# A transformer block with its gradients on one core: a written order for SP's queue, other places for weight loads, and q's row bound made earlier

## The chip, the core and the metric

The kernel runs on one core of a Trainium2 chip. The metric is device time in microseconds from launch to end; lower is better. The program is one launch with all inputs and outputs in device memory. A profiled execution gives, beside its own time, a span: from its first to its last instruction.

## What is computed

The reference is a block with attention beside a gated feed-forward part, and all of its gradients:

```
xn = layernorm(x)                                   # x: 1 x 2048 x 512
q, k, v = split(xn @ wqkv)                          # 32 heads of 16
s = softmax(q k^T / 4) v, heads joined, @ wo
b = gelu(layernorm(xn) @ w1 + b1) @ w2 + b2         # 512 -> 1792 -> 512
out = x + s * silu(b)
returns out and the gradients of x, wqkv, wo, w1, b1, w2, b2 for a given grad_out
```

Data are bfloat16. Gelu is the tanh form. No maximum is subtracted from the scores as they come: each row of q gets a bound, minus the root of (its squared norm times the largest squared norm of a k row of that head), which is put into an extra column of q so that the score matmul subtracts it.

## The kernel before, in words

The work has three parts: a part before attention (`phase_pre`, L42 to L481), attention forward and backward together (`attention_core`), and the remaining gradients (`phase3`). The change touches only the first and its hand-over to the second.

**Data.** The 2048 rows are 16 tiles of 128 rows; four tiles are a group. Group g is loaded as one 128 x 4 x 512 tile. Tiles are named as in the code: x4 (input), xn4 (normalized), y4 (normalized twice), xnT and yT (their transposes), NS (k and v), NQ (q, with an extra column for the bound), KPad and QPad (padded copies that are transposed for attention), ND (grad_out-side operand of attention), h1p (before Gelu), hgT (after it), dso4 (gradient that enters attention), gB (gate and its gradient), do4 (grad_out).

**Stages, in the order of TensorE.** (1) Layer norm, and per tile the projections to k, v and q (`kv_tile`, 12 matmuls). The transposes xnT of groups 0 and 1 are made by TensorE (`turn_xn`), those of groups 2 and 3 and all yT by DMA transposes on SP's queue (L134, L163). ScalarE (ACT) copies the results out of PSUM. (2) For groups 0 and 1, `h_tile(g, fc)`: 14 tiles of 4 matmuls each, with the bias added by VectorE (DVE, L267) for even fc and for 5 and 11, by ACT (L269) for the others; every second tile ACT applies Gelu (L271) and two stores are issued on SP's queue: H1T_s (L272) and HGT_s (L273). (3) `m_group(0)`: per row tile 14 matmuls with w2 (L282), then on DVE and ACT the gate: m = result + b2 (L286), tanh and sigmoid (L289, L290), gB and dso (L294, L295; dso reads do4), and three operations more (L304 to L309), with a store of gB by GpSimd (POOL, L310). At the end of a group dso4 is transposed by DMA (L299) and stored. `m_group` begins with `load_do`, the load of do4, of which there is one buffer. (4) `h_tile` of group 2, with `do_proj` (a matmul with wo's transpose, cast by ACT to ND, L346) behind its last four tiles; m_group(1); the same for group 3; m_group(2). The last group's m, and the do_proj of groups 2 and 3, are left over: `left_over` hands them out as steps that stand in the first block of attention.

PSUM has seven banks in this part, shared by all matmul results (`psA`, tag "mm"); one more is the pool `psz`.

**Norms and the bound.** `norms` squares a tile on POOL (L174, two buffers named sq) and sums it on DVE (L175): `k_norm` for k in stage 1, `q_norm` for q in the h stages (after fc 2, 4, 6, 8, 10, 12 of group 1; 1, 3, 5, 6, 8, 9 of group 2; 1, 3, 5, 6 of group 3). The maximum over all k rows is made in h of group 0: DVE reduces over tiles (L453), then POOL over partitions (`partition_all_reduce`, L454). Then `row_shift1` multiplies the norms (L434, L435; after fc 9 of group 3), `row_shift2` takes the root on ACT (L439; after its last fc), and `row_shift3` writes NQ's column, copies it to QPad on POOL and transposes (`turn_q`, L426), behind h of group 3.

**What sets the order.** Inside a `tc.manual_schedule(engines=...)` block, the named engines run their instructions in the order of the code. In both blocks of `phase_pre` these are TensorE, ACT, DVE and POOL. SP, which only issues DMAs, is not among them: its order is chosen by the framework's scheduler, which may put an instruction ahead of others that stand before it in the code. Each queue works strictly in order; an instruction that waits for a semaphore holds up what is behind it. In the built program SP's order is: x(0), x(1), w2, the transpose of wo, b1, XN_s(0), x(2), XN_s(1), x(3), and then the stage's transposes and stores in the code's order; the transpose of KPad (L460) and the loads of b2 and do (group 0) come before the first H1T_s; the loads of do for groups 1 and 2 come five DMAs ahead of the last HGT_s of the h stage before them. ACT's queue issues the loads of wqkv (two parts) and w1 at the start.

Of the kernel before, what the change touches and what calls it, by code (L numbers as in the profile page):

```python
# [9 lines left out]
f32 = mybir.dt.float32  # L10
# [26 lines left out]
def rows4(a, g):  # L37

    return a[g * 512:(g + 1) * 512].rearrange("(p t) d -> p t d", t=4)


def phase_pre(ctx, tc, k, A_x, A_wqkv, A_wo, B_w1, B_b1, B_w2, B_b2, grad_out, opnds, psz, tailp):  # L42
# [25 lines left out]
    nc.vector.memset(half[:], 0.5)  # L68
    kmaxrun = wts.tile([128, H], f32, name="kmaxrun")
    kmax2 = wts.tile([128, H], f32, name="kmax2")  # L70

    yT, hgT = {}, {}
    c2 = c1.enter_context(ExitStack())
    p1 = pool(c2, "pre_p1", 2)
    wqkv_sb = p1.tile([128, IC, 3 * D], bf16, name="wqkv_sb", bufs=1)
# [4 lines left out]
    def load_x(g):  # L80
        x4[g] = p1.tile([128, 4, D], bf16, name="x4", bufs=2)
        if g == 0:
            for h in range(2):
                nc.sync.dma_start(out=x4[g][64 * h:64 * h + 64], in_=rows4(x2, g)[64 * h:64 * h + 64])
        else:
            nc.sync.dma_start(out=x4[g][:], in_=rows4(x2, g))

# [82 lines left out]
        nc.scalar.activation(out=dst, in_=ps[:].rearrange("p (a j c) -> p a j c", a=NPAIR, j=2), func=ACT.Copy, scale=0.25 if c0 == 0 else 1.0)  # L170

    def norms(pl, dst, src):
        sq = pl.tile([128, H, DH], f32, name="sq", bufs=2)
        nc.gpsimd.tensor_tensor(out=sq[:].rearrange("p (a j) c -> p a j c", j=2), in0=src, in1=src, op=ALU.mult)  # L174
        nc.vector.reduce_sum(out=dst, in_=sq[:], axis=AX.X)  # L175

# [20 lines left out]
    def k_norm(g, i):  # L197
        norms(p1, kn2[:, 4 * g + i, :], NS[g][:, :, i, :, 1:17])

    with tc.manual_schedule(engines={ET_.PE, ET_.Activation, ET_.DVE, ET_.Pool}):  # L200
        for g in range(2):
            load_x(g)
        nc.scalar.dma_start(out=wqkv_sb[:, :, D:3 * D], in_=wq3[:, :, D:3 * D])
        nc.scalar.dma_start(out=wqkv_sb[:, :, 0:D], in_=wq3[:, :, 0:D])
        nc.scalar.dma_start(out=w1_sb[:], in_=B_w1.rearrange("(c p) f -> p c f", p=128))
        for g in range(4):
            NS[g] = p1.tile([128, NPAIR, 4, 2, NATW], bf16, name="NS", bufs=4)
            nc.gpsimd.memset(NS[g][:, :, :, :, 0:1], 1.0)
        open1(0)
        open1(1)  # L210
        one_a(0, 0)
        for i in range(4):
            one_a(*divmod(i + 1, 4))
            one_b(0, i)
            turn_xn(0, i)
        load_x(2)
        for i in range(4):
            if i < 3:
                one_a(1, i + 1)
            one_b(1, i)  # L220
            if i == 3:
                n2_a(0)
            kv_tile(0, i)
            turn_xn(1, i)
        load_x(3)
        for h4 in range(4):
            permuted_kv(h4)
        steps = [(root2, 0), (n1_a, 2), (n2_b, 0), (kv_tile, 1, 0), (root1, 2), (n2_c, 0, 0), (n2_c, 0, 1), (n1_b, 2),
                 (kv_tile, 1, 1), (n2_c, 0, 2), (n2_c, 0, 3), (n2_a, 1), (kv_tile, 1, 2), (root2, 1), (n1_a, 3), (n2_b, 1),
                 (kv_tile, 1, 3), (root1, 3), (n1_b, 3), (n2_c, 1, 0), (n2_c, 1, 1), (kv_tile, 2, 0), (n2_a, 2), (n2_c, 1, 2),  # L230
                 (n2_c, 1, 3), (kv_tile, 2, 1), (root2, 2), (k_norm, 0, 0), (k_norm, 0, 1), (n2_b, 2), (kv_tile, 2, 2),
                 (n2_c, 2, 0), (n2_c, 2, 1), (k_norm, 0, 2), (k_norm, 0, 3), (n2_a, 3), (kv_tile, 2, 3), (n2_c, 2, 2),
                 (n2_c, 2, 3), (root2, 3), (n2_b, 3), (kv_tile, 3, 0)] + [(k_norm, 1, i) for i in range(4)]
        steps += [(n2_c, 3, 0), (n2_c, 3, 1), (kv_tile, 3, 1), (k_norm, 2, 0), (k_norm, 2, 1), (n2_c, 3, 2), (n2_c, 3, 3),
                  (kv_tile, 3, 2), (k_norm, 2, 2), (k_norm, 2, 3), (k_norm, 3, 0), (k_norm, 3, 1), (kv_tile, 3, 3), (k_norm, 3, 2), (k_norm, 3, 3)]
        for f, *a in steps:
            f(*a)
# [2 lines left out]
    p2 = pool(c1, "pre_p2", 2)  # L240
    h1ps = [p2.tile([128, 2, 512], bf16, name="h1p", bufs=6)]
    w2_sb = k.Oall[:].rearrange("p t d -> p (t d)")[:, 0:FC * D].rearrange("p (c d) -> p c d", c=FC)
    nc.sync.dma_start(out=w2_sb, in_=B_w2.rearrange("(c p) d -> p c d", p=128))
    nc.sync.dma_start_transpose(out=woT, in_=A_wo)
    qn2 = p2.tile([128, NT, H], f32, name="qn2", bufs=1)
    b2_bf = p2.tile([128, D], bf16, name="b2_bf", bufs=1)
    nc.sync.dma_start(out=b2_bf[:], in_=B_b2.rearrange("(o d) -> o d", o=1).to_broadcast([128, D]))
    nc.gpsimd.tensor_copy(out=b2f[:], in_=b2_bf[:])
    nc.sync.dma_start(out=b1_bf[:], in_=B_b1.rearrange("(c p) -> p c", p=128))
    nc.gpsimd.tensor_copy(out=b1c[:], in_=b1_bf[:])  # L250
    ND, dsoT, dso4, do4 = {}, {}, {}, {}

    def h_tile(g, fc):
# [96 lines left out]
    def do_done(g):  # L350
        ts = slice(4 * g, 4 * g + 4)
        nd0 = ND[g][:, 0].rearrange("p t (j c) -> p t j c", j=2)
        nc.gpsimd.tensor_copy(out=QPad[:, ts, 2:4, 0:16], in_=nd0)
        if g >= 2:
            turn_q(g)
        nc.sync.dma_start(out=k.NATQd_s[g], in_=ND[g])
        nc.gpsimd.tensor_copy(out=OP0["NATQd"][:, ts], in_=nd0)

    def left_over(big, mid2, xt2, st2):
# [60 lines left out]
            steps[2 * n + 3][0].append((rest2, t))  # L420
        for g, f in ((8, (do, 8)), (9, (do, 10)), (10, (turn, 0)), (11, (do, 12)), (12, (do, 14))):
            steps[g][1].append(f)
        return steps

    def turn_q(g):
# [15 lines left out]
    def row_shift3():  # L441
        for ts in (slice(0, 4), slice(4, 16)):
            nc.vector.tensor_scalar(out=NQ[:, :, ts, :, 0], in0=qn2[:, ts].rearrange("p t (a j) -> p a t j", j=2), scalar1=-1.0, scalar2=None,
                                    op0=ALU.mult)
            nc.gpsimd.tensor_copy(out=QPad[:, ts, 0:2, 0:17], in_=NQ[:, 0, ts])
            turn_q(ts.start // 4)
        nc.gpsimd.tensor_copy(out=OP0["NATQq"][:], in_=NQ[:, 0])

    with tc.manual_schedule(engines={ET_.PE, ET_.Activation, ET_.DVE, ET_.Pool}):
        for fc in range(FC):  # L450
            h_tile(0, fc)
            if fc == 5:
                nc.vector.reduce_max(out=kmaxrun[:], in_=kn2[:].rearrange("p t h -> p h t"), axis=AX.X)  # L453
                nc.gpsimd.partition_all_reduce(kmax2[:], kmaxrun[:], channels=128, reduce_op=bass_isa.ReduceOp.max)  # L454
        qn = list(range(NT))
        for fc in range(FC):
            h_tile(1, fc)
            if fc in (2, 4, 6, 8, 10, 12):
                q_norm(qn.pop(0))
        nc.sync.dma_start_transpose(out=OP0["KVT"][:].rearrange("r (m k) -> r m k", m=16), in_=KPad[:].rearrange("q k s c -> q (k s c)"))  # L460
        m_group(0)
        for g in (2, 3):
            for fc in range(FC):
                h_tile(g, fc)
                if g == 3 and fc == 9:
                    row_shift1()
                if g == 3 and fc == FC - 1:
                    row_shift2()
                if fc >= 10:
                    do_proj(4 * (g - 2) + fc - 10)  # L470
                elif fc in (1, 3, 5, 6) or fc in (8, 9) and g == 2:
                    q_norm(qn.pop(0))
            if g == 2:
                m_group(1)
        e_one = p2.tile([128, 1], f32, name="e_one", bufs=1)
        nc.scalar.activation(out=e_one[:], in_=k.eps_t[:], func=ACT.Exp)
        row_shift3()
        m_group(2)
        nc.sync.dma_start(out=k.NATQq_s, in_=NQ[:].rearrange("p a t j c -> p a (t j c)"))
    c1.close()  # L480
# [806 lines left out]
```

## Time and profile before

| | |
|---|---|
| time, median of 3 runs | 2342.68 us (2340.48 to 2344.0) |
| the profiled execution | 2337.01 us, of which the span is 2335.1 us |
| PE busy (matmul) | 2228.5 us, 95% of the span |
| DVE, ACT, POOL busy | 2024.3, 2043.9, 315.3 us |
| before attention (to TensorE's first score matmul) | 166.7 us |
| granted TensorE clock, mean | 0.988 |
| DMA traffic | 415.56 MB, 178 GB/s |

How to read it: the busy times overlap, since the engines run side by side. A line of a timeline has the start in us from the beginning of the span, the time taken, the engine, the line of the code, the operation, what is written and read, the count of equal instructions merged and, in brackets, how long the engine stood idle before and what ended that. An engine's name with a q (SPq) is its queue, where DMAs are issued; their landing comes later. "DMA share" is the mean busy share of the 16 DMA engines; values over 1 are edges of stretches. The profiled execution lies 5.7 us under the median of the runs.

### The profile page before, as it was taken

How to read it: one execution, taken by the hardware profiler on the slowest of the kernel's cores; microseconds unless marked ns; L12 is line 12 of the kernel's file. 1: busy time of each engine (PE TensorE's matmuls, PEld its weight loads, DVE VectorE, ACT ScalarE, POOL GpSimd, SP SyncE). 2: the span in 40 equal slices, each digit the busy share in tenths (PEclk: the TensorE clock that was granted, in tenths of full speed). 3: DMA queues.
4: the chain of work that ended last, by engine and by line, in shares of the span. 5: the costliest groups of instructions: out<-in, count | busy, mean ns of one | idle time of the engine just before them, and what ended most of it. 6: DMA issues, size and time to landing. Idle time of an engine off the chain costs nothing.

```text
span 2335.1 us, 50892 instructions
## 1 busy us (share of the span) xinstructions
PE 2228.5 (95%) x20082; PEld 795.2 (34%) x20128; DVE 2024.3 (87%) x3601; ACT 2043.9 (88%) x2329; POOL 315.3 (14%) x758
## 2 busy tenths in 40 slices
PE   7888999999999999999999999999999998889698
PEld 3333333333333333333333333333333333334344
DVE  6577999999999999999999999999999996775164
ACT  6566999999999999999999999999999998883143
POOL 4321111111111111111111111111111112100000
PEclk9999999999999999999999999999999999999899
DMA  9788999999999999999999999999999898796961
GB/s 295 228 279 176 170 179 163 187 157 186 164 180 164 181 165 177 170 173 178 167 180 162 186 162 180 168 179 164 178 169 176 159 157 221 192 214 123 184 163 64
DMA packets 1315362, 415.56 MB, mean 178 GB/s; under 512 B 1272241, under 2 KB 1291698, under 8 KB 1313970
## 3 DMA queue, kind: packets, MB, share of 16 engines
q1 hardware_dynamic: 1311362, 401.56, 90.7%
q0 software_dynamic: 2176, 7.34, 0.9%
q8 instruction: 157, 2.57, 0.4%
q10 hardware_dynamic: 1584, 3.41, 0.4%
q14 instruction: 83, 0.68, 0.1%
HBM read 46.52 MB, written 49.03 MB: 41 GB/s over the span
## 4 chain that ended last, share of the span: by engine, by line
PE 77%; DVE 10%; ACT 3%; issue 3%; DMA 3%; SPq 2%; POOL 0%; DVEq 0%; ACTq 0%; POOLq 0%
PE d L916 12%; PE X L953 11%; PE s L894 11%; PE Z L1034 9%; PE X L966 7%; DVE gts L933 5%; PE Z L1026 5%; PE t L906 5%; PE ET L878 5%; PE XT L978 2%; PE ps_dw L661 1%; PE X L956 1%; PE ps_dhg L676 1%; PE ps_dy L716 1%; PE ps_dwkv L766 1%
## 5 line engine op out<-in xcount | busy, mean ns | idle before, releaser
L933 DVE TENSOR_TENSOR gts<-d,et 128x512 bf16<-128x512 f32 x2048 | 1322.0, 684 | 71.4 <-PE d L916 22.0
L922 ACT ACTIVATE et<-s 128x1024 bf16<-128x1024 f32 x1024 | 1044.6, 1046 | 8.8 <-PE d L916 7.5
L927 ACT ACTIVATE e<-t 128x1024 bf16<-128x1024 f32 x832 | 867.5, 1043 | 23.1 <-PE t L906 5.4
L916 PE MATMUL d<-QDT,KVT 32*128 32x512 bf16 x2048 | 756.5, 384 | 18.7 <-DVE gts L933 17.5
L894 PE MATMUL s<-QDT,KVT 32*128 32x512 bf16 x2048 | 398.3, 384 | 4.8 <-ACT et L922 2.7
L1034 PE MATMUL Z<-gk,W 128*32 128x512 bf16 x2048 | 397.1, 384 | 0.0
L953 PE MATMUL X<-et,Lc 128*32 128x512 bf16 x2048 | 370.1, 389 | 0.0
L956 PE MATMUL X<-et,NAT 128*32 128x512 bf16 x2048 | 368.9, 388 | 0.0
L966 PE MATMUL X<-gts,NAT 128*17 128x512 bf16 x2048 | 330.5, 381 | 0.0
L906 PE MATMUL t<-KVT,QDT 32*128 32x512 bf16 x1664 | 323.7, 384 | 0.9 <-ACT e L927 0.9
L1026 PE MATMUL Z<-e,W 128*32 128x512 bf16 x1664 | 321.6, 383 | 2.7 <-DVE ob L1053 1.2
L916 PEld LDWEIGHTS <-KVT 32*128 32x128 bf16 x2048 | 173.2, 91 | 235.1 <-issue 234.7
L894 PEld LDWEIGHTS <-KVT 32*128 32x128 bf16 x2048 | 105.9, 91 | 249.1 <-issue 229.3
L1000 POOL TENSOR_TENSOR W<-NATQd,rL 128x128 bf16<-128x128 bf16 x64 | 25.7, 401 | 1120.8 <-DVE rL L999 1120.8
L1034 PEld LDWEIGHTS <-W 128*32 128x32 bf16 x2048 | 100.3, 95 | 172.5 <-issue 142.0
L906 PEld LDWEIGHTS <-QDT 32*128 32x128 bf16 x1664 | 92.5, 91 | 146.1 <-issue 141.0
L1026 PEld LDWEIGHTS <-W 128*32 128x32 bf16 x2048 | 105.2, 94 | 105.7 <-issue 96.6
L953 PEld LDWEIGHTS <-Lc 128*32 128x32 bf16 x2048 | 83.6, 93 | 162.3 <-issue 162.2
L883 DVE COPY eE<-ET 128x1024 bf16<-128x1024 bf16 x192 | 130.1, 678 | 4.4 <-PE ET L878 4.4
L878 PE MATMUL ET<-ident_bf,et 128*128 128x128 bf16 x1536 | 119.1, 220 | 2.1 <-DVE e L286 2.1
L878 PEld LDWEIGHTS <-et 128*128 128x128 bf16 x1536 | 86.5, 98 | 45.6 <-issue 45.6
L966 PEld LDWEIGHTS <-NAT 128*17 128x17 bf16 x2048 | 79.6, 89 | 59.4 <-issue 42.8
(197 smaller groups left out, 2328.6 us busy)
## 6 DMA issues: line engine op xcount, KB each, us to landing
gk<-gts SPq DMA_TRANSPOSE x512, 4.5
H1T_s<-h1p SPq DMA_DIRECT2D x28, 256.0 KB, 4.2
h<-H1T_s SPq DMA_DIRECT2D x28, 256.0 KB, 3.3
HGT_s<-hgT SPq DMA_DIRECT2D x21, 256.0 KB, 4.4
NAT_s<-NS SPq DMA_DIRECT2D x4, 1056.0 KB, 5.9
dKVT_s<-ob SPq DMA_DIRECT2D x16, 256.0 KB, 3.6
gb<-GB_s SPq DMA_DIRECT2D x4, 1024.0 KB, 5.8
Rkv<-dKVT_s SPq DMA_DIRECT2D x2, 2048.0 KB, 14.1
```

The source lines that it names most:

```text
L878: nc.tensor.transpose(ET[:, hj, m * 128:(m + 1) * 128], st_et[g - 3 + m][:, hj, 384:512], ident_bf[:])
L894: nc.tensor.matmul(s[:, hj, :], lhsT=op["KVT"][r, kb * 128:(kb + 1) * 128], rhs=op["QDT"][r, qc * 512:(qc + 1) * 512], start=True, stop=Tr ...
L906: nc.tensor.matmul(t[:, hj, :], lhsT=op["QDT"][r, q0:q0 + 128], rhs=op["KVT"][r, kc * 512:(kc + 1) * 512], start=True, stop=True, tile_pos ...
L916: nc.tensor.matmul(d[:], lhsT=op["KVT"][r, kb * 128:(kb + 1) * 128], rhs=op["QDT"][r, qc * 512:(qc + 1) * 512], start=True, stop=True, til ...
L922: nc.scalar.activation(out=et[:], in_=st_s.pop(g)[:], func=ACT.Exp)
L927: nc.scalar.activation(out=e[:], in_=st_t.pop(g)[:], func=ACT.Exp)
L933: nc.vector.tensor_tensor(out=gts[:, g % 2, hj], in0=st_d.pop((g, hj))[:], in1=st_et[g][:, hj], op=ALU.mult)
L953: nc.tensor.matmul(X[64 + 32 * hj:96 + 32 * hj, :], lhsT=Lc[:, :], rhs=et[:, hj, :], start=(kb == 0), stop=False, skip_group_check=True, t ...
L956: nc.tensor.matmul(X[32 * hj:32 * hj + 32, :], lhsT=NATt[:, kb, hj, 1:33], rhs=et[:, hj, :], start=(kb == 0), stop=(kb == 15), tile_positi ...
L966: nc.tensor.matmul(X[64 + 32 * hj:64 + 32 * hj + 17, :], lhsT=NATt[:, kb, hj, 0:17], rhs=gts[:, kb % 2, hj, :], start=False, stop=(kb == 1 ...
L1026: nc.tensor.matmul(Z[32 * hj:32 * hj + 32, :], lhsT=blk[j]["W1"][:, qb, hj, :], rhs=e[:, hj, :], start=(qb == 0), stop=False, tile_positio ...
L1034: nc.tensor.matmul(cur["Z"][32 * hj:32 * hj + 32, :], lhsT=blk[j]["W2"][:, qb, hj, :], rhs=grhs, start=False, stop=(qb == 3), tile_positio ...
```

## The change

SP joins the engines with a written order, in both blocks. Its instructions therefore stand in the order of the code, and the code moves several of them. x(0) is loaded as its first row tile and the other three, no longer as two halves of the partitions. wqkv comes as three parts, in the order k, v, q; w1 and b1 are asked for in the middle of stage 1; w2 on ACT's queue at the head of the second block's code; b2 behind tile 1 of h of group 0; wo's transpose right before m_group(0); KPad's right before m_group(1).

The maximum of k's squares over partitions is made by TensorE in three steps behind fc 5, 8 and 11 of group 0 (`k_max`): a transpose, a reduction and a diagonal matrix on DVE, and a matmul with ones that spreads the 32 maxima over all partitions. POOL's reduction goes.

The q norms move: after fc 0 to 3 and 5 to 8 of group 2, and 0 and 1 of group 3. `row_shift1`, 2 and 3 now stand behind fc 3, 5 and 9 of group 3; of `row_shift3` only the first four tiles are transposed there, and `do_done` transposes those of the other groups. The first sq of this part is allocated at its head. In the first block of attention, the last step gets two fills of two matmuls each, whose results nobody reads.

In the built program w2's load stands on ACT's queue behind the second root of stage 1. do for group 0 stands behind HGT_s of h of group 1's last pair and wo's transpose; do for group 1 behind the last HGT_s of group 2, NATQd_s and KPad's transpose; do for group 2 behind the last HGT_s of group 3, a transpose of QPad and NATQd_s.

```diff
@@ -68,8 +68,12 @@
     nc.vector.memset(half[:], 0.5)
     kmaxrun = wts.tile([128, H], f32, name="kmaxrun")
     kmax2 = wts.tile([128, H], f32, name="kmax2")
-
-    yT, hgT = {}, {}
+    kmd = wts.tile([H, H], f32, name="kmd")
+    kmt = wts.tile([H, 1], f32, name="kmt")
+    ones_h = wts.tile([H, 128], f32, name="ones_h")
+    nc.gpsimd.memset(ones_h[:], 1.0)
+
+    yT, hgT, sqs = {}, {}, []
     c2 = c1.enter_context(ExitStack())
     p1 = pool(c2, "pre_p1", 2)
     wqkv_sb = p1.tile([128, IC, 3 * D], bf16, name="wqkv_sb", bufs=1)
@@ -80,8 +84,8 @@
     def load_x(g):
         x4[g] = p1.tile([128, 4, D], bf16, name="x4", bufs=2)
         if g == 0:
-            for h in range(2):
-                nc.sync.dma_start(out=x4[g][64 * h:64 * h + 64], in_=rows4(x2, g)[64 * h:64 * h + 64])
+            for ts in (slice(0, 1), slice(1, 4)):
+                nc.sync.dma_start(out=x4[g][:, ts], in_=rows4(x2, g)[:, ts])
         else:
             nc.sync.dma_start(out=x4[g][:], in_=rows4(x2, g))
 
@@ -170,7 +174,7 @@
         nc.scalar.activation(out=dst, in_=ps[:].rearrange("p (a j c) -> p a j c", a=NPAIR, j=2), func=ACT.Copy, scale=0.25 if c0 == 0 else 1.0)
 
     def norms(pl, dst, src):
-        sq = pl.tile([128, H, DH], f32, name="sq", bufs=2)
+        sq = sqs.pop() if sqs else pl.tile([128, H, DH], f32, name="sq", bufs=2)
         nc.gpsimd.tensor_tensor(out=sq[:].rearrange("p (a j) c -> p a j c", j=2), in0=src, in1=src, op=ALU.mult)
         nc.vector.reduce_sum(out=dst, in_=sq[:], axis=AX.X)
 
@@ -197,12 +201,11 @@
     def k_norm(g, i):
         norms(p1, kn2[:, 4 * g + i, :], NS[g][:, :, i, :, 1:17])
 
-    with tc.manual_schedule(engines={ET_.PE, ET_.Activation, ET_.DVE, ET_.Pool}):
+    with tc.manual_schedule(engines={ET_.PE, ET_.Activation, ET_.DVE, ET_.Pool, ET_.SP}):
         for g in range(2):
             load_x(g)
-        nc.scalar.dma_start(out=wqkv_sb[:, :, D:3 * D], in_=wq3[:, :, D:3 * D])
-        nc.scalar.dma_start(out=wqkv_sb[:, :, 0:D], in_=wq3[:, :, 0:D])
-        nc.scalar.dma_start(out=w1_sb[:], in_=B_w1.rearrange("(c p) f -> p c f", p=128))
+        for v in (1, 2, 0):
+            nc.scalar.dma_start(out=wqkv_sb[:, :, v * D:(v + 1) * D], in_=wq3[:, :, v * D:(v + 1) * D])
         for g in range(4):
             NS[g] = p1.tile([128, NPAIR, 4, 2, NATW], bf16, name="NS", bufs=4)
             nc.gpsimd.memset(NS[g][:, :, :, :, 0:1], 1.0)
@@ -223,6 +226,9 @@
             kv_tile(0, i)
             turn_xn(1, i)
         load_x(3)
+        nc.scalar.dma_start(out=w1_sb[:], in_=B_w1.rearrange("(c p) f -> p c f", p=128))
+        nc.sync.dma_start(out=b1_bf[:], in_=B_b1.rearrange("(c p) -> p c", p=128))
+        nc.gpsimd.tensor_copy(out=b1c[:], in_=b1_bf[:])
         for h4 in range(4):
             permuted_kv(h4)
         steps = [(root2, 0), (n1_a, 2), (n2_b, 0), (kv_tile, 1, 0), (root1, 2), (n2_c, 0, 0), (n2_c, 0, 1), (n1_b, 2),
@@ -240,14 +246,9 @@
     p2 = pool(c1, "pre_p2", 2)
     h1ps = [p2.tile([128, 2, 512], bf16, name="h1p", bufs=6)]
     w2_sb = k.Oall[:].rearrange("p t d -> p (t d)")[:, 0:FC * D].rearrange("p (c d) -> p c d", c=FC)
-    nc.sync.dma_start(out=w2_sb, in_=B_w2.rearrange("(c p) d -> p c d", p=128))
-    nc.sync.dma_start_transpose(out=woT, in_=A_wo)
+    sqs = [p2.tile([128, H, DH], f32, name="sq", bufs=2)]
     qn2 = p2.tile([128, NT, H], f32, name="qn2", bufs=1)
     b2_bf = p2.tile([128, D], bf16, name="b2_bf", bufs=1)
-    nc.sync.dma_start(out=b2_bf[:], in_=B_b2.rearrange("(o d) -> o d", o=1).to_broadcast([128, D]))
-    nc.gpsimd.tensor_copy(out=b2f[:], in_=b2_bf[:])
-    nc.sync.dma_start(out=b1_bf[:], in_=B_b1.rearrange("(c p) -> p c", p=128))
-    nc.gpsimd.tensor_copy(out=b1c[:], in_=b1_bf[:])
     ND, dsoT, dso4, do4 = {}, {}, {}, {}
 
     def h_tile(g, fc):
@@ -351,7 +352,7 @@
         ts = slice(4 * g, 4 * g + 4)
         nd0 = ND[g][:, 0].rearrange("p t (j c) -> p t j c", j=2)
         nc.gpsimd.tensor_copy(out=QPad[:, ts, 2:4, 0:16], in_=nd0)
-        if g >= 2:
+        if g >= 1:
             turn_q(g)
         nc.sync.dma_start(out=k.NATQd_s[g], in_=ND[g])
         nc.gpsimd.tensor_copy(out=OP0["NATQd"][:, ts], in_=nd0)
@@ -420,6 +421,12 @@
             steps[2 * n + 3][0].append((rest2, t))
         for g, f in ((8, (do, 8)), (9, (do, 10)), (10, (turn, 0)), (11, (do, 12)), (12, (do, 14))):
             steps[g][1].append(f)
+        def fill(_):
+            w = z("fill")
+            for n in range(2):
+                nc.tensor.matmul(w[:], lhsT=woT[:, 0, 0:128], rhs=woT[:, 0, :], start=(n == 0), stop=(n == 1))
+        steps[13][0].append((fill, 0))
+        steps[13][1].append((fill, 0))
         return steps
 
     def turn_q(g):
@@ -443,38 +450,58 @@
             nc.vector.tensor_scalar(out=NQ[:, :, ts, :, 0], in0=qn2[:, ts].rearrange("p t (a j) -> p a t j", j=2), scalar1=-1.0, scalar2=None,
                                     op0=ALU.mult)
             nc.gpsimd.tensor_copy(out=QPad[:, ts, 0:2, 0:17], in_=NQ[:, 0, ts])
-            turn_q(ts.start // 4)
+            if ts.start == 0:
+                turn_q(0)
         nc.gpsimd.tensor_copy(out=OP0["NATQq"][:], in_=NQ[:, 0])
 
-    with tc.manual_schedule(engines={ET_.PE, ET_.Activation, ET_.DVE, ET_.Pool}):
+    def k_max(n):
+
+        if n == 0:
+            nc.vector.reduce_max(out=kmaxrun[:], in_=kn2[:].rearrange("p t h -> p h t"), axis=AX.X)
+        elif n == 1:
+            k_max.ps = psA.tile([128, 512], f32, name="ps_km", tag="mm")
+            nc.tensor.transpose(k_max.ps[0:H, 0:128], kmaxrun[:], k.ident_f[:])
+            nc.vector.reduce_max(out=kmt[:], in_=k_max.ps[0:H, 0:128], axis=AX.X)
+            nc.vector.tensor_scalar(out=kmd[:], in0=k.ident_f[0:H, 0:H], scalar1=kmt[:, 0:1], scalar2=None, op0=ALU.mult)
+        else:
+            ps = psA.tile([128, 512], f32, name="ps_kb", tag="mm")
+            nc.tensor.matmul(ps[:, 0:H], lhsT=ones_h[:], rhs=kmd[:], start=True, stop=True)
+            nc.vector.tensor_copy(out=kmax2[:], in_=ps[:, 0:H])
+
+    with tc.manual_schedule(engines={ET_.PE, ET_.Activation, ET_.DVE, ET_.Pool, ET_.SP}):
+        nc.scalar.dma_start(out=w2_sb, in_=B_w2.rearrange("(c p) d -> p c d", p=128))
         for fc in range(FC):
             h_tile(0, fc)
-            if fc == 5:
-                nc.vector.reduce_max(out=kmaxrun[:], in_=kn2[:].rearrange("p t h -> p h t"), axis=AX.X)
-                nc.gpsimd.partition_all_reduce(kmax2[:], kmaxrun[:], channels=128, reduce_op=bass_isa.ReduceOp.max)
+            if fc in (5, 8, 11):
+                k_max((fc - 5) // 3)
+            if fc == 1:
+                nc.sync.dma_start(out=b2_bf[:], in_=B_b2.rearrange("(o d) -> o d", o=1).to_broadcast([128, D]))
+                nc.gpsimd.tensor_copy(out=b2f[:], in_=b2_bf[:])
         qn = list(range(NT))
         for fc in range(FC):
             h_tile(1, fc)
             if fc in (2, 4, 6, 8, 10, 12):
                 q_norm(qn.pop(0))
-        nc.sync.dma_start_transpose(out=OP0["KVT"][:].rearrange("r (m k) -> r m k", m=16), in_=KPad[:].rearrange("q k s c -> q (k s c)"))
+        nc.sync.dma_start_transpose(out=woT, in_=A_wo)
         m_group(0)
         for g in (2, 3):
             for fc in range(FC):
                 h_tile(g, fc)
+                if g == 2 and fc < 9 and fc != 4 or g == 3 and fc in (0, 1):
+                    q_norm(qn.pop(0))
+                if g == 3 and fc == 3:
+                    row_shift1()
+                if g == 3 and fc == 5:
+                    row_shift2()
                 if g == 3 and fc == 9:
-                    row_shift1()
-                if g == 3 and fc == FC - 1:
-                    row_shift2()
+                    row_shift3()
                 if fc >= 10:
                     do_proj(4 * (g - 2) + fc - 10)
-                elif fc in (1, 3, 5, 6) or fc in (8, 9) and g == 2:
-                    q_norm(qn.pop(0))
             if g == 2:
+                nc.sync.dma_start_transpose(out=OP0["KVT"][:].rearrange("r (m k) -> r m k", m=16), in_=KPad[:].rearrange("q k s c -> q (k s c)"))
                 m_group(1)
         e_one = p2.tile([128, 1], f32, name="e_one", bufs=1)
         nc.scalar.activation(out=e_one[:], in_=k.eps_t[:], func=ACT.Exp)
-        row_shift3()
         m_group(2)
         nc.sync.dma_start(out=k.NATQq_s, in_=NQ[:].rearrange("p a t j c -> p a (t j c)"))
     c1.close()
```

## The prediction

> **What bounds the kernel now.** I read the page first: the span, and the chain that ended last.
>
> ```profile
> span 2335.1 us, 50892 instructions
> PE 77%; DVE 10%; ACT 3%; issue 3%; DMA 3%; SPq 2%; POOL 0%; DVEq 0%; ACTq 0%; POOLq 0%
> ```
>
> TensorE carries the span, but the change touches only the part before attention. So the second view is the busy time by stretches, cut where TensorE changes stage: start, projections, h of groups 0 and 1, m of group 0 with h of group 2, m of group 1 with h of group 3, the crossing into attention, attention.
>
> ```profile
> 0.00:15.40 15.40, 2.16 (x16) 1.37 (x17) 6.32 (x21) 4.21 (x9) 6.89 (x16) 1.00 0.92 293
> 15.40:63.50 48.10, 45.55 (x208) 20.52 (x209) 37.83 (x94) 40.55 (x77) 25.09 (x37) 0.96 1.04 291
> 63.50:97.70 34.20, 26.62 (x113) 11.35 (x112) 16.34 (x25) 18.59 (x23) 10.52 (x15) 0.90 0.83 265
> 97.70:126.10 28.40, 27.98 (x126) 12.51 (x128) 23.58 (x43) 17.89 (x24) 8.94 (x11) 1.00 0.65 222
> 126.10:166.70 40.60, 40.17 (x182) 17.90 (x183) 27.15 (x53) 27.94 (x40) 9.84 (x16) 1.00 0.77 255
> 166.70:230.50 63.80, 50.58 (x352) 17.31 (x356) 47.69 (x89) 39.05 (x44) 6.33 (x15) 0.89 0.82 193
> ```
>
> The columns after the length are the busy times of PE, PEld, DVE, ACT and POOL, the granted clock, the DMA share and GB/s. TensorE fills all stages but three: the start (nothing has landed), the third (26.62 of 34.20) and the crossing. In the projections the DMA engines are full (1.04) beside a full TensorE. The timeline shows the hole of the third:
>
> ```profile
> 83.10 0.45 POOL L454 PARTITION_ALL_REDUCE kmax<-kmaxrun  x1 [5.73 <-DVE h1p L267]
> 90.85 2.03 POOL L174 TENSOR_TENSOR sq<-NQ 128x512 f32<-128x512 bf16 x2 [7.30 <-DMA HGT_s<-hgT]
> 91.91 0.69 DVE L175 TENSOR_REDUCE qn<-sq 128x32 f32<-128x512 f32 x1 [8.99 <-POOL sq L174]
> 93.31 4.56 PE L264 MATMUL ps_h<-yT,w_sb 128*128 128x512 bf16 x12 [7.15 <-DVE h1p L267]
> ```
>
> POOL shows 0.45 us of reduction, but from the end of its last cast (77.36) to 90.85 it does nothing else. The first q_norm waits behind it, DVE stands 8.99 us in line behind that norm, and TensorE 7.15. The store named as releaser is no cause: sq's waits in the built program are for two old stores of NS.
>
> Then the loads of grad_out (do), which the change moves; timeline rows of SP's queue and DVE:
>
> ```profile
> 72.55 0.42 SPq L317 DMA_DIRECT2D do<-in_grad_out_dram  x1
> 101.69 0.51 SPq L273 DMA_DIRECT2D HGT_s<-hgT  x1
> 105.01 0.43 DVE L295 TENSOR_TENSOR dso<-do,gB 128x512 bf16<-128x512 bf16 x1
> 124.25 0.75 SPq L317 DMA_DIRECT2D do<-in_grad_out_dram  x1
> 129.25 0.34 SPq L273 DMA_DIRECT2D HGT_s<-hgT  x1
> 133.42 0.42 DVE L295 TENSOR_TENSOR dso<-do,gB 128x512 bf16<-128x512 bf16 x1
> 152.68 0.63 SPq L317 DMA_DIRECT2D do<-in_grad_out_dram  x1
> ```
>
> Today each load is asked for 9 to 32 us before DVE needs it, ahead of stores that stand before it in the code. With SP in the code's order, the built program has it behind the last HGT_s store of the h stage before, and behind one transpose more.
>
> **The change part by part.** Times are the profiled execution's: 2337.01 us, span 2335.1. The median of the runs is 2342.68, 5.7 above it; the sum is a difference, and I add it to the median.
>
> *k's maximum.* The hole goes: 7.15 us, and the 12 matmuls behind it, which took 4.56 us where 12 x 0.2167 = 2.60 are due (the clock was 0.50 there): 9.1. Ends: 7.2 (the idle alone), and 9.9 (34.2 less 112 x 0.2167). What replaces it is two small matmuls and three small DVE operations, 0.17 to 1.0 us each by L434 and L453; in h DVE has some 8 us free, so I cost them at nothing, or 1 us if it had not. **-9.1.**
>
> *Start.* DVE's first work waits until 8.86 for x, two 256 KB halves (6.9 us to land). Now 128 KB come first, then 384. The rate there is about 360 GB/s, shared by two queues: the first part might land near 5, the rest near 7.2. From tile 1 on DVE paces the turns (1.31 us each), so TensorE starts some 2.5 us earlier (none to 3.9). But w1, 1.8 MB, is now asked behind the last turn's copy (28.70, so about 26 us), into the projections where the DMA share is 1.04; x(2) and XN_s(0), 1.0 MB, leave that stretch forwards. The rest is 0.8 MB, 2.1 us at 380 GB/s; nothing to 4.7 us (all of w1). xnT(3) already ends TensorE's longest wait there (2.34 us at 51.44). Both: **-0.5**, -3.9 to +4.7. w2 doesn't go near its stage: the built program issues it on ACT after the second root, at some 8 us.
>
> *do(0).* Before, the last HGT_s is asked 3.98 us after TensorE begins m of group 0 (97.71). Behind it now stand wo's transpose and then do. No row shows wo's alone: the 17.63 us of 3.27 lie under the whole start. Lower end: w2T's 7.46 us for 3.5 times as much, so 2.1; upper: KVT's 5.94 behind a full queue. I take 2.5, near dsoT's 2.79 and 2.49 in the same stage. do lands 5.5 us after its issue (5.3 to 5.5 in three rows; 3.8 for a DSO_s store of its size). 3.98 + 0.51 + 2.5 + 5.5 = 12.5, and DVE wants it at 7.3 (105.01 - 97.71): 5.2 late (3.1 to 8.6). Queued behind the waiting dso on DVE are 20 operations of m, then h1p of group 2; TensorE then waits for a PSUM bank. It has no reserve: it already stands 0.23 us at 119.89 and again at 148.31 for h1p. **+5.2.**
>
> *Two more norms early in h of group 2.* Norms now follow tiles 0 and 1, so h1p of tile 2 falls one POOL-DVE turn back (1.04 + 0.68, 1.1 net) and that of tile 4 two. **+2.2** (0 to 3.0, the price if POOL hands over one by one).
>
> *do(1).* Last HGT_s 129.25, NATQd_s to 130.48, KVT's transpose 2.5 (1.9 to 5.9), do 5.5: 138.5 against 133.42. **+5.1** (2.8 to 8.5), passed on as above.
>
> *Row bound within h of group 3, and do(2).* The Sqrt now lies between Gelus: one more table load, 1.28 us, on an ACT that is full from 148.94 on. The two norms and the row factor put h1p of tiles 4 and 5 1.3 us back, and with it Gelu. So ND's last cast ends at 162.4, not 159.81. Behind it on SP: POOL's copy 0.3, turn_q 1.2, NATQd_s 0.35, then do at 164.3, landed 169.8; DVE had begun this dso at 163.09. From there DVE works back to back until the first gts of attention (173.05). **+6.7** (3.7 with a landing in 3.8 us and no DVE delay; 9 with a transpose of 3.5). What the row shift freed at 159 to 161 is worth nothing, since do ends last.
>
> The Trainium skill speaks against this place ("ScalarE: Activation LUTs", Rules for kernel authors): do all of one table set before switching. Its section on what ACT_TABLE_LOAD costs gives about 1.28 us for the load and 1.38 for a drain. The rows agree with the load and not with the drain: loaded from 157.41, Sqrt begins at 158.71. By the page the sum would be 1.4 us longer.
>
> *Fill.* Four matmuls, 0.87 us at most. They stand at the end of the first block; at 219 to 226 the clock is 0.50 to 0.71 and a matmul takes 0.60 us for 0.39. If that goes and TensorE paced those 7.2 us, 2.5 come back; DVE has gaps there too. **-0.8** (-2.6 to +0.9).
>
> Sum: -9.1 - 0.5 + 5.2 + 2.2 + 5.1 + 6.7 - 0.8 = **+8.8 us**, so 2345.8 for the profiled execution and **2351.5** for a median. Attention and what follows it run in the same order on TensorE but for these.
>
> **Rivals.**
> 1. *The banks carry it: faster.* Seven PSUM banks let TensorE run ahead while DVE waits for do, and DVE regains the time in h of groups 2 and 3 (11.5 us of work under 15.6 of TensorE). Then do(0), do(1) and the norms cost nothing and only the end pays: -9.1 - 0.5 - 0.8 + 3.7 to 6.7 = -6.7 to -3.7, about 2337.5. It decides if TensorE never stands over 1 us at tile 8 of those h stages. For it: slack on average. Against: the two waits of 0.23. Chance 0.25.
> 2. *The projections pay for w1.* xnT(2), asked near 31 and needed near 36 (33.72 and 38.58 before, less 2.5), lands late, and all behind it on SP's queue: +4.7 in place of -0.5, so +14.0, 2356.7. For it: the share of 1.04; against: slack at 32 to 36 (0.72). Chance 0.15.
> The Trainium skill states the rule behind this one ("DMA: Bandwidth & Descriptors", Issuing engines are not separate DMA queues): DMAs of all engines run on the same 16 engines and interleave. The trace agrees: in the first 20 us the ACT and SP queues took 51.9% and 43.3%.
> 3. *It cancels.* The do loads land in 3.8 us and the transposes in 2 us, so that 3.1 + 2.8 + 3.7 stand against 10.4 with 1 to 2 us for the norms: +0.7, 2343. For it: the DMA engines are idle in much of m (0.03 at 104 to 108). Chance 0.15.
> 4. *It doesn't do what it says*: w2, asked at 8 us, holds up x and wqkv as before and nothing moves at the start: 2.5 us worse than the sum, 2354. Chance 0.05.
>
> The forecast keeps 0.4.
>
> **Range and chances.** The ends of all terms together reach from -7 to +28, but not all stand at one end; from rival 1's far end to about two thirds of the upper part is -6.7 to +20.3: 2336 to 2363. A measurement of this kernel tells about 0.2%, 4.7 us. Faster by more: 0.14 of rival 1 and 0.03 of the third, 0.17. Within: 0.11 of rival 1, 0.10 of the third, 0.02 of the forecast, 0.23. Slower by more: the rest, 0.60.
>
> **What would show it.** No idle of some 7 us on TensorE in h of group 1. A wait of DVE's dso for do in all three m groups, 3 to 8 us each; if these rows are missing, the forecast falls. PE waits for h1p at tile 8 of h of groups 2 and 3. A second Gelu load near 153. In the projections a longer wait for xnT(2) speaks for rival 2. The first gts some 9 us later than 173.05.

## The result, and the profile after

The changed kernel takes 2366.83 us (median; 2364.26 to 2370.12) where the kernel before, run beside it, takes 2342.61: a ratio of 1.0105 (95% interval 1.0087 to 1.0122), 24.2 us slower. The forecast had slower, by 8.8 us; the time lies 3.8 us above the upper end of its range. The profiled execution took 2370.12 us, 3.3 above its median, that of before 5.6 below; so the two traces are compared up to one mark, the first matmul of the rows left over for attention (`ps_m` out of dQall), behind which TensorE's order is the same but for the fills. It stands at 175.79 us before and at 199.52 after: 23.73 us, nearly the whole difference of the medians. The spans of the two traces differ by 33.2 us, 9.5 more than at the mark; 8.9 of these are the distances of the two executions from their medians.

The page and the busy time by stretches, cut where TensorE changes stage in this kernel as before (start, projections, h of groups 0 and 1, m0 with h2, m1 with h3 and m2, crossing):

```profile
span 2368.3 us, 50906 instructions
PE 75%; DVE 12%; DMA 4%; ACT 3%; issue 3%; SPq 2%; POOL 1%; DVEq 0%; ACTq 0%
```
```profile
0.00:12.10 12.10, 2.15 (x16) 1.37 (x17) 6.54 (x21) 4.21 (x9) 7.05 (x17) 1.00 0.84 286
12.10:67.90 55.80, 48.52 (x208) 21.07 (x211) 35.32 (x90) 39.20 (x73) 21.63 (x33) 0.91 0.95 260
67.90:95.30 27.40, 24.99 (x116) 11.19 (x115) 20.67 (x33) 21.77 (x29) 12.83 (x16) 1.00 0.87 300
95.30:128.90 33.60, 30.01 (x127) 12.78 (x129) 23.34 (x43) 16.61 (x22) 10.36 (x12) 0.95 0.72 220
128.90:175.80 46.90, 42.03 (x184) 18.11 (x186) 22.77 (x43) 28.08 (x39) 8.57 (x15) 0.96 0.65 210
175.80:254.20 78.40, 50.94 (x371) 17.85 (x376) 52.25 (x98) 41.09 (x47) 6.91 (x16) 0.85 0.70 167
```

The start is 3.3 us shorter and the third stretch has lost its hole (34.20 to 27.40). Every other stretch is longer: projections 48.10 to 55.80, the two m and h stages 28.40 to 33.60 and 40.60 to 46.90, the crossing 63.80 to 78.40. TensorE's timeline says what it waited for:

```profile
39.76 1.89 PE L173 MATMUL pk<-wqkv_sb,xnT 128*128 128x512 bf16 x4 [4.43 <-DMA xnT<-xn]
59.30 1.86 PE L173 MATMUL pv<-wqkv_sb,xnT 128*128 128x512 bf16 x4 [2.27 <-ACT NS L174]
78.39 0.27 PE L463 MATMUL ps_km<-ident_f,kmaxrun 128*32 128x128 f32 x1 [1.96 <-DVE kmaxrun L460]
116.96 1.50 PE L265 MATMUL ps_h<-yT,w_sb 128*128 128x512 bf16 x4 [2.27 <-DVE h1p L268]
197.86 1.18 PE L943 MATMUL d<-QDT,KVT 32*128 32x512 bf16 x2 [13.88 <-DVE gts L960]
```

**Crossing.** The longest wait was not forecast. The tile view of NATQq_s names who waited for this store of 2.2 MB out of NQ; the timelines of SP, ACT and DVE say when, first those of the kernel before, then those of the changed one:

```profile
163.90 0.53 SPq L479 DMA_DIRECT2D NATQq_s<-NQ  x1
169.87 3.08 ACT L922 ACTIVATE et<-s 128x1024 bf16<-128x1024 f32 x3
```
```profile
187.59 0.43 SPq L506 DMA_DIRECT2D NATQq_s<-NQ  x1
197.10 1.02 ACT L949 ACTIVATE et<-s 128x1024 bf16<-128x1024 f32 x1 [13.78 <-DMA NATQq_s<-NQ]
197.12 1.29 DVE L960 TENSOR_TENSOR gts<-d,et 128x512 bf16<-128x512 f32 x2 [11.50 <-DMA NATQq_s<-NQ]
```

In both built programs ACT's second et and DVE's first gts wait for this store: the memory that the program gives to them is part of what NQ had held, so the store has to have read NQ first. Before, SP issued it at 163.90, ahead of code that stands before it; it landed 7.0 us later, at 170.9, just when ACT came to its second et (the three et of 169.87 follow one another without a gap). In the written order it stands behind the transpose and the store of dso of group 2, which wait for DVE's last dso: 187.59, landed 9.4 us later. DVE had ended its own work of this part at 185.6.

**Projections.** xnT of group 2 is late (4.43 us) and the 16 matmuls behind it run from 39.76 to 46.13, at half clock most of the time (6.4 us where 3.5 are due). The wait of 2.27 us has a chain of its own; the row of each engine that hands it on:

```profile
38.20 0.20 POOL L231 CAST b1c<-b_bf 128x14 f32<-128x14 bf16 x1 [12.97 <-DMA b_bf<-in_B_b_dram]
54.17 0.69 DVE L179 TENSOR_REDUCE kn<-sq 128x32 f32<-128x512 f32 x1 [9.44 <-POOL sq L178]
57.23 1.52 ACT L164 ACTIVATE y<-xn,nms,rstd 128x512 bf16<-128x512 bf16 x2 [5.99 <-DVE nms L156]
```

b1, 3.5 KB, asked for at 27.15 beside w1's 1.8 MB, lands 11 us later. Its cast is ahead of POOL's packing of wkva, all but the first of KPad's copies, and the squares of k; DVE stands in order for the squares, ACT for DVE's nms, TensorE for ACT's copies out of PSUM. The same lateness of k's norms makes the 1.96 us at 78.39.

**do.** DVE's dso waits in all three m groups, as forecast:

```profile
106.15 0.43 DVE L296 TENSOR_TENSOR dso<-do,gB 128x512 bf16<-128x512 bf16 x1 [3.55 <-DMA do<-in_grad_out_dram]
140.41 0.42 DVE L296 TENSOR_TENSOR dso<-do,gB 128x512 bf16<-128x512 bf16 x1 [4.26 <-DMA do<-in_grad_out_dram]
175.53 0.42 DVE L296 TENSOR_TENSOR dso<-do,gB 128x512 bf16<-128x512 bf16 x1 [3.21 <-DMA do<-in_grad_out_dram]
```

### The profile page after: what moved, and what is told of

It reads as the page before. It is cut to its first block, busy times and chain, and to the rows that moved or that the text cites. A ratio compares the mean times of both kernels' runs of the same rounds, so it can differ in the third digit from the quotient of the medians.

```text
span 2368.3 us, 50906 instructions
## 1 busy us (share of the span) xinstructions
PE 2239.0 (95%) x20089; PEld 798.1 (34%) x20135; DVE 2025.8 (86%) x3604; ACT 2046.5 (86%) x2330; POOL 314.8 (13%) x758
## 4 chain that ended last, share of the span: by engine, by line
PE 75%; DVE 12%; DMA 4%; ACT 3%; issue 3%; SPq 2%; POOL 1%; DVEq 0%; ACTq 0%
PE d L943 12%; PE X L980 11%; PE s L921 10%; PE Z L1061 9%; PE X L993 7%; DVE gts L960 5%; PE Z L1053 5%; PE t L933 4%; PE ET L905 4%; PE XT L1005 2%; PE ps_dw L688 2%; PE X L983 1%; PE ps_dhg L703 1%; PE ps_dy L743 1%; PE ps_dwkv L793 1%
```

## The experiments

One table holds all runs. Columns: the time over that of the kernel before on the same chip (its median stands in the last column), then, from the one profile of each run, in us, TensorE's first matmul of h, the length of h of groups 0 and 1 (h0+h1), of m of group 0 with h of group 2 (m0+h2), of m1 with h3, and of the crossing (first score matmul to the mark), and the mark itself. m of group 2 (12.2 us in all) is left out.

| run | ratio (95%) | h at | h0+h1 | m0+h2 | m1+h3 | crossing | mark | median, before's |
|---|---|---|---|---|---|---|---|---|
| before | 1 | 63.50 | 34.21 | 28.40 | 28.42 | 9.08 | 175.79 | |
| after | 1.0105 (1.0087 to 1.0122) | 67.89 | 27.45 | 33.54 | 34.72 | 23.74 | 199.52 | 2366.83, 2342.61 |
| e1 store | 1.0050 (1.0037 to 1.0064) | 67.87 | 27.46 | 33.02 | 35.06 | 12.21 | 187.81 | 2349.95, 2339.27 |
| e2 b1 | 1.0088 (1.0073 to 1.0102) | 63.55 | 27.24 | 33.76 | 34.65 | 24.06 | 195.45 | 2359.72, 2339.27 |
| e3 w1 | 1.0077 (1.0063 to 1.0091) | 63.95 | 24.88 | 32.27 | 34.63 | 24.14 | 192.05 | 2357.66, 2339.27 |
| e4 do | 1.0065 (1.0051 to 1.0080) | 68.62 | 27.48 | 30.25 | 31.61 | 20.62 | 190.76 | 2353.70, 2339.27 |
| e5 all four | 0.9980 (0.9971 to 0.9989) | 62.10 | 25.58 | 30.25 | 31.65 | 9.93 | 171.69 | 2338.14, 2342.88 |
| e6 k's maximum | 0.9968 (0.9955 to 0.9981) | 63.19 | 28.34 | 28.41 | 28.41 | 9.10 | 169.64 | 2335.36, 2342.88 |
| e7 SP's order | 1.0072 (1.0060 to 1.0084) | 63.09 | 33.01 | 33.11 | 28.83 | 25.15 | 195.37 | 2359.41, 2342.88 |
| e8 norms back | 0.9950 (0.9938 to 0.9962) | 61.68 | 25.42 | 28.42 | 28.74 | 9.06 | 165.50 | 2331.45, 2342.88 |
| e9 SP free | 0.9950 (0.9937 to 0.9962) | 63.48 | 25.61 | 28.42 | 28.41 | 9.06 | 167.16 | 2332.83, 2343.39 |
| e10 no fill | 0.9958 (0.9944 to 0.9971) | 61.89 | 25.37 | 28.41 | 28.93 | 9.10 | 165.89 | 2333.32, 2343.39 |
| e11 row bound back | 0.9967 (0.9954 to 0.9979) | 62.81 | 25.26 | 30.26 | 29.77 | 9.02 | 169.31 | 2336.16, 2343.39 |

My theory after the traces: four places on the queues lose the time (the store of NATQq, b1, w1, do), and the parts of the change that compute are worth what they show. The rival: one late thing, above all do, is behind all of it, and the other waits are only last names.

**e1: the store alone.** Edit (m_group, and the line removed at the end):

```diff
         load_do(g)
+        if g == 2:
+            nc.sync.dma_start(out=k.NATQq_s, in_=NQ[:].rearrange("p a t j c -> p a (t j c)"))
```

> The changed kernel, with one store moved: NATQq_s (2.2 MB, out of NQ) is asked for right behind the load of do of group 2, and no longer behind the transpose and the store of dso of that group. In the profile of the changed kernel ACT's second et and DVE's first gts stand 13.8 and 11.5 us until this store has landed (197.06), and in the program both wait for its semaphore, since attention's buffers lie where NQ lay. Theory (the store is the gate): asked near 172, it lands near 181; TensorE's idle of 13.9 us before the first d falls to about 2 and the first d starts near 186, so 11 to 12 us are won: about 2355. Rival (the late do of group 2 is the gate, the store only the last name on the wait): the first gts is held by DVE's chain anyway, under 3 us are won, 2364 to 2367. A half-way case: the store's 2.2 MB share the DMA engines with do, which lands 3 us later: about 2358.

```profile
171.37 0.85 SPq L325 DMA_DIRECT2D NATQq_s<-NQ  x1
185.82 0.58 PE L944 MATMUL d<-QDT,KVT 32*128 32x512 bf16 x1 [1.38 <-DVE gts L961]
```

The first d comes at 185.82, as expected, the mark 11.71 us earlier. The store was the gate; that do of group 2 landed later beside it (DVE's wait 4.19 for 3.21) cost no more than 1 us. What is left of the crossing over before (12.21 for 9.08) is do's, as e4 shows.

**e2: b1 alone, e3: w1 alone.** Edits: e2 puts b1's load behind the loop of `load_x` at the head; e3 puts w1's load into the loop over the first group's tiles:

```diff
             turn_xn(0, i)
+            if i == 0:
+                nc.scalar.dma_start(out=w1_sb[:], in_=B_w1.rearrange("(c p) f -> p c f", p=128))
```

> The changed kernel, with only the load of b1 (3.5 KB) moved: on SP's queue behind x(1), as one of the first, and no longer behind x(3) and beside w1. Theory (b1 holds up POOL, and POOL the rest): POOL's cast of b1, which waited 12.97 us until 38.20, stands ahead of the packing of wkva, KPad's copies and the squares of k; with b1 there early, DVE's 9.44 us wait for sq, ACT's 5.99 us for nms and TensorE's 2.27 us at 59.3 go, and so do its 0.45 and 1.96 us in h of group 0: 4 to 7 us won, 2360 to 2363. The wait for xnT of group 2 (4.43 us) stays. Rival (w1's 1.8 MB in the middle of the projections cost all of it by themselves): nothing changes, 2367.

> The changed kernel, with only the load of w1 moved: on ACT's queue behind the copy of the first transposed tile (near 9 us) and no longer behind that of (1,3) at 25.0. In the changed kernel the DMA engines are at 0.50 and 0.26 of their time from 15 to 25 us. Theory (w1 in the projections costs): TensorE's wait for xnT of group 2 (4.43 us, and some 3 us of matmuls at half clock behind it) goes, x(3) lands sooner, and b1, alone on the engines, no longer holds POOL: 9 to 12 us won, 2355 to 2358. Rival 1 (b1's place is all): POOL's wait goes, the wait for xnT stays: 2361. Rival 2 (xnT of group 2 is late because of its own place on SP's queue): wait unchanged, 2364 to 2367.

TensorE's timeline, of e2, then of e3, then POOL's of e3:

```profile
40.33 1.88 PE L173 MATMUL pk<-wqkv_sb,xnT 128*128 128x512 bf16 x4 [4.24 <-DMA xnT<-xn]
72.44 0.27 PE L463 MATMUL ps_km<-ident_f,kmaxrun 128*32 128x128 f32 x1 [0.96 <-DVE kmaxrun L460]
75.68 1.02 PE L265 MATMUL ps_h<-yT,w_sb 128*128 128x512 bf16 x4 [1.24 <-ACT h1p L270]
```
```profile
50.74 1.89 PE L173 MATMUL pk<-wqkv_sb,xnT 128*128 128x512 bf16 x4 [4.45 <-DMA xnT<-xn]
```
```profile
33.69 0.20 POOL L232 CAST b1c<-b_bf 128x14 f32<-128x14 bf16 x1 [7.91 <-DMA b_bf<-in_B_b_dram]
```

b1 alone wins 4.07 us by the mark, all in the projections: POOL's wait and TensorE's at 59.3 are gone, the one for xnT of group 2 stays, as expected; that h of group 0 would gain too was wrong (27.24): the wait for k's norms shrinks to 0.96 us, but another of 1.24 us takes its place, for ACT, whose first Gelu waits 6.30 us until the store NAT_s of group 3 has landed. w1 alone wins 7.47, less than I expected: xnT of group 2 is in time, but b1, though no longer beside w1, still holds POOL for 7.91 us, and xnT of group 3 comes 4.45 late. So these are two mechanisms. In e3 the Gelu's wait for NAT_s is 3.34 us and TensorE has no wait in h of group 0 (24.88). Both together (e5) bring h to 62.10.

b1 is few bytes but not a small load: in the first 12.5 us of e2 the DMA engines move 1905 packets of under 512 bytes, in those of the changed kernel, without b1, 97. In the kernel before, while b1 is under way, they move 1445 packets from 22.38 to 23.30 us and are busy 0.86 of that time, at 3 GB/s.

**e4: do alone.** Edit: the tile and its load out of `m_group` into `ask_do(g)`, called behind tile 1 of h of group 0 and tile 9 of h of groups 2 and 3.

> The changed kernel, with only the loads of do moved ahead on SP's queue: group 0 behind tile 1 of h of group 0, groups 1 and 2 behind tile 9 of the h stage before their m, about where they stood before. DVE's waits for do (3.55, 4.26 and 3.21 us) go. Theory (late do passes on to TensorE in full): 9 to 11 us won, 2356 to 2358, and TensorE's 2.27 us waits in h of groups 2 and 3 go. Rival (the seven PSUM banks carry it; the waits in h of groups 2 and 3 come from the two early q norms): only the last, 3.2 us, is won, which also puts the NATQq store forwards: 2363, and the 2.27 us waits stay.

TensorE's timeline of e4, in h of group 2, where the wait of 2.27 us at tile 8 is gone and this one at tile 10 is left, and at the crossing:

```profile
118.03 1.02 PE L265 MATMUL ps_h<-yT,w_sb 128*128 128x512 bf16 x4 [0.88 <-DVE h1p L268]
189.10 1.18 PE L948 MATMUL d<-QDT,KVT 32*128 32x512 bf16 x2 [13.90 <-DVE gts L965]
```

8.76 us by the mark, a little under what was expected. DVE's waits are gone, and m0+h2 and m1+h3 fall by 3.29 and 3.11, the crossing by 3.12: late do passes on to TensorE for the most part (of 3.55, 4.26 and 3.21). The banks do not carry it; the rival falls, and with it the first rival of the prediction. The store is still the gate at the crossing (13.90). What stays over the kernel before is 1.85 and 3.19 us.

**e5 and e8: all four, and the norms back.** e5 has the edits of e2, e3, e4, and the store ahead of `m_group(2)`. e8 also has the q norms and the row bound where they were before.

> The changed kernel with the four places of the runs before at once: b1 behind x(1), w1 behind the first transposed tile, do of the three groups ahead as before the change, and NATQq_s ahead of m of group 2. What is left of the change: SP in the order of the code, x(0) in row tiles, wqkv in three parts, k's maximum by TensorE, the early q norms, the row bound within h of group 3, the fills. Theory (the four places are the loss): by the first matmul of the rows left over for attention, the four alone won 11.71, 4.07, 7.47 and 8.76 us of the 23.73 that the change had lost there; b1's and w1's gains are largely the same one, so 25 to 28 us together: the marker comes 2 to 4 us before that of the kernel before, and the time is 2335 to 2338 where the kernel before takes 2339. Rival (gains overlap, since do of group 2 and the store end the same wait): 20 to 22 us, still 2 to 4 us slower than before, 2341 to 2344.

> The run with four places put back, and in addition the q norms and the three steps of the row bound at the places of the kernel before. Theory (the early norms and the root between the Gelus cost): with do early, m of group 0 with h of group 2 took 1.85 us more and m of group 1 with h of group 3 took 3.19 us more than before; both go, 4 to 5.5 us won on the run with four places back, about 2331 to 2333. Rival (the row bound's early place gains at the crossing what it costs in h): within 2 us of the run with four places back.

e5's mark is 4.10 us ahead of before: the four places together win 27.83 us, as expected. The single runs of the store, do and w1 come to 27.9 (11.71 + 8.76 + 7.47), so these gains hardly overlap; that of b1 (4.07) lies mostly within w1's. e8 wins 6.19 more and beats both kernels: 0.9950. In it the hole's stretch has shrunk to 25.42 us, where its 112 matmuls need 24.3 (busy time by stretches):

```profile
61.68:87.10 25.42, 24.88 (x116) 11.27 (x115) 18.79 (x30) 19.19 (x24) 9.52 (x12) 1.00 0.97 323
```

**e11: row bound back, norms early.** e5 with the three steps of the row bound at their old places.

> The run with four places put back, with the three steps of the row bound at the places of the kernel before, and the q norms left early. It parts the 6.2 us that norms and row bound cost together by the first matmul of the left-over rows (171.69 against 165.50). Theory (the root between the Gelus, with its extra Gelu table load of 1.28 us on a full ACT, costs most in h of group 3, the two more norms the 1.8 us in h of group 2): 3 to 4 us won, marker 167.5 to 168.5, time 2334 to 2335. Rival (the norms cost in both stages): 1 to 2 us won, 2336 to 2337.

2.38 us by the mark, between the two, with the rival's time; that the norms cost in both stages is the rival's part too. From e5 to e11 the row bound's place gives 1.88 us in h3 and 0.91 at the crossing, from e11 to e8 the norms' 1.84 in h2 and 1.03 in h3; the rest lies at the start, where these runs differ by up to 1.1 us although none of them changes anything there.

**e6: k's maximum alone, in the kernel before.** `k_max` in three steps in place of POOL's reduction.

> The kernel before with one part of the change: k's maximum over partitions by TensorE in three steps, no reduction by POOL. Theory (the hole of POOL is worth what it shows): TensorE's 7.15 us of idle and the 12 slow matmuls behind it go, h of groups 0 and 1 takes 25 us and not 34.21: 8 to 9.5 us won, 2330 to 2331.5. Rival (the hole hides a later wait: stores of h, do or the lanes of SP, since SP's order is the scheduler's and shifts): 4 us or less, 2335.

In between: 6.15 us by the mark. ACT's and TensorE's timelines, of before, then of e6:

```profile
71.28 1.28 ACT L271 ACT_TABLE_LOAD   x1 [5.12 <-DVE h1p L267]
74.26 7.24 PE L264 MATMUL ps_h<-yT,w_sb 128*128 128x512 bf16 x32 [0.24 <-ACT h1p L269]
```
```profile
71.75 1.28 ACT L275 ACT_TABLE_LOAD   x1 [5.89 <-DMA NAT_s<-NS]
74.73 1.02 PE L268 MATMUL ps_h<-yT,w_sb 128*128 128x512 bf16 x4 [1.77 <-ACT h1p L273]
```

In e6 ACT's first Gelu waits until NAT_s of group 3, the store out of NS, has landed; before, it was nearly as late (71.28). But before, TensorE has run twelve tiles of h when it comes to ACT's late h1p, and waits 0.24 us; in e6 it has run eleven and waits 1.77: in both the wait stands at the thirteenth PSUM tile of the stage, and in e6 ps_km is one of them (seven banks are shared). Behind it TensorE ran with a granted clock of 0.58 and 0.56 from 76 to 80 us behind it. So the three steps are not free where ACT is late. In e8, where the table load stands at 69.01, 7.3 us behind the first matmul of h and not 8.6, 0.54 us are left of the wait.

**e7: SP's order alone, in the kernel before.** Edit: SP in both lists of engines, nothing else.

> The kernel before with one word added in two places: SP among the engines with a written order; nothing else is moved in the code. On SP's queue that puts KPad's transpose and do of group 0 behind the last HGT_s of h of group 1, do of groups 1 and 2 behind the last HGT_s and NATQd_s, and NATQq_s behind the transpose and store of dso of group 2. Theory (the order alone loses what the change lost in m, h of groups 2 and 3 and the crossing): 3.3 us for do of group 0, 3.1 for group 1, 12 to 15 at the crossing: 18 to 21 us slower than before, 2357 to 2360. Rival (it was the moved loads and norms that lost, and the order itself is harmless): 2339 to 2343.

```profile
193.71 1.18 PE L916 MATMUL d<-QDT,KVT 32*128 32x512 bf16 x2 [13.86 <-DVE gts L933]
```

19.58 us by the mark, 16.9 by the ratio: the order alone does most of the harm, and the wait for the store is the same as in the changed kernel. The crossing (+16.1) and do of group 0 (+4.7) lose a little more than expected, h of groups 0 and 1 gains 1.2; do of group 1, with no transpose ahead of it, costs 0.4 and not 3.1.

**e9 and e10: is the written order, is the fill worth anything?** e9 is e8 with SP out of the lists again, e10 is e8 without the fills.

> The run with the norms put back, with SP taken out of the engines with a written order again, so that the framework's scheduler chooses SP's order; nothing else. In the built program wo's transpose then stands among the first loads, KPad's transpose and do of group 0 ahead of the first H1T_s. Theory (the written order had no worth of its own: what it moved cost time, and put back it only stands level): within 3 us of that run, 2329 to 2334. Rival 1 (the written order gains: KPad's transpose and wo's, kept out of the projections and of the Gelu's start, are worth 2.6 us at xnT and 2 to 3 us in h of group 0, as with k's maximum alone, where h of groups 0 and 1 took 28.34 us against 25.42): 3 to 5 us slower, 2334.5 to 2336.5.

> The run with the norms put back, without the two fills of two matmuls each in the last step of the first block of attention. Theory (the fills change nothing that can be measured: the four matmuls are 0.87 us at most, and the slow clock behind the crossing came in the changed kernel as before): within 1.5 us, 2330 to 2333. Rival (they keep the clock up): 2 to 3 us slower without them, 2333.5 to 2334.5, and lower granted clock behind the last pd.

e9 can't be told from e8 in time: that a good written order is better than the scheduler's is not shown. (By the mark e9 comes 1.66 us later, all of it before h; single traces differ there by up to 1.1.) e10 differs by 0.0008, within both intervals. The granted clock does differ, behind the last pd, in e8 and in e10 (it stands third from the end):

```profile
205.50:215.50 10.00, 8.19 (x75) 2.62 (x76) 7.97 (x13) 9.17 (x10) 1.20 (x3) 1.00 0.93 195
```
```profile
205.89:215.89 10.00, 8.16 (x57) 2.40 (x53) 7.56 (x12) 8.78 (x9) 1.20 (x3) 0.71 0.99 199
```

The clock buys something, and it is lost again: with the fills the next eight transposes of et begin 53.55 us behind the mark, without them 54.87. In e8 TensorE then stands 1.26 us for POOL's W, and the transposes after these begin at 62.29 and 62.41.

## Why the prediction was wrong, point by point

Forecast +8.8, of which +9.6 by the mark, since the fills stand behind it; measured by the mark +23.7. Each term with what replaced it:

- **k's maximum, -9.1: measured -6.8** in the change, -9.3 in e3. Right about the hole. Wrong was the cost of nothing for its three steps: TensorE waited 1.96 us for k's norms in the change, 0.96 for them and 1.24 for ACT with b1 early (e2), 1.77 for ACT where the steps were the only change (e6, -5.9). Without such waits (e3) the term is what was forecast.
- **Start and w1, -0.5: measured +4.4.** The start gave -3.3, the projections +7.7. The price of w1 was rival 2's mechanism; that the sum comes near its 4.7 is in part luck, since that had no gain at the start. The forecast had taken w1 at 2.1 us of added traffic. The working followed the bytes and not the small load among them: b1's new place was never priced, though POOL's cast stands ahead of nearly all that POOL does in the projections; alone it is worth 4.1 us (e2).
- **do of group 0 and two early norms, 5.2 + 2.2: measured 5.1**, of which the norms 1.85 and do 3.3 (e4). do was there 10.8 us behind the first matmul of m, not 12.5: the last HGT_s was asked 1.5 us sooner and the load took 4.0 us for 5.5, while wo's transpose took 3.7 for 2.5.
- **do of group 1, 5.1, and row bound with do of group 2, 6.7: together 11.8, measured 21.0** (6.3 in m1+h3, 14.7 at the crossing). do of group 1 gave 3.1, do of group 2 3.1 (it was there 11.9 us behind the first matmul of its m, where the forecast has 15.3), norms and row bound in h3 3.2, and the rest is the store. The step that failed is the sentence "From there DVE works back to back until the first gts of attention (173.05)", which makes do of group 2 the last thing that the first gts waits for. DVE did work back to back, to 185.6, and then stood 11.5 us: NATQq_s, which the written order moves too, stands in no term of the sum and was not followed to who waits for it. It cost 11.5 us at the crossing (e1), half of the whole loss. The first gts came at 197.12, 24 us later than 173.05 and not 9.
- **Fill, -0.8: nothing measurable in time** (e10); 1.3 us in the trace, of which 0.1 is left nine us later.

The misses add up: 4.9 + 2.3 - 2.3 + 9.2 = 14.1, the distance from 9.6 to 23.7. The sign was right, and do was the mechanism that it was said to be; with the store at its 11.5 us the sum would have been 20.3 and the median 2363. The Trainium skill's rule of rival 2 ("DMA: Bandwidth & Descriptors", Issuing engines are not separate DMA queues) agrees with the runs: with w1 asked for on ACT's queue at 25 us, the transpose of xn of group 2 on SP's queue kept TensorE waiting 4.43 and 4.24 us (after, e2), with w1 at 8.5 us not at all (e3).

## What to carry to other kernels

When a queue gets a written order, list every transfer that the scheduler had put ahead of its code, and follow each to its last waiter; a store's waiter may be whoever gets its source's memory next, and no operand names it. Price a load by its packets and by who stands in order behind its first reader, not by its bytes: 3.5 KB cost 4 us here. Place loads by measured idle stretches of the DMA engines (here w1 and b1 were asked for before 10 us). Moving the norms and the row bound forwards within the h stages lost 5.7 us here (e5 to e8).

## What the runs showed of the hardware

- A short stand of TensorE can halve its clock: behind the 2.27 us at 59.30 the granted clock was 0.51 until 62.4, behind the 4.43 us at 39.76 it was 0.50 until 45.0. Its length alone doesn't decide: behind the 1.77 us of e6 the clock fell to 0.58, behind the 1.96 us at 78.39 it stayed at 1.00. A wait of 4.43 us cost 7.5 us: the first matmul came 4.6 us late, and 16 took 6.4 us for 3.5. The Trainium skill ("TensorE: Matmul & The Clock Gate", What's actually happening) puts the window of idleness that brings the half clock at about 3.4 us; here 2.27 us was followed by it.
- The 3.5 KB of b1 took 11 us to land beside w1 (DMA share 1.13 from 27 to 38 us), and 3.4 us in the kernel before, where the share was 1.09 as well (20.96 to 24.4): the share alone does not tell how long a load takes.
- The store of 2.2 MB landed in 7.0 us before, and in 9.4 us after and 9.7 in e1, where a load of 512 KB of grad_out was asked for within 0.6 us of it.
